# Moving the output scaling later, and five smaller edits, in a fused attention and two-layer kernel on one Trainium2 core

## The chip, the cores and the metric

The kernel runs on one core of a Trainium2 chip. The metric is the device time of one execution in microseconds (us). Each kernel was run several times on the same chip as the kernel before. A ratio is the mean time of one kernel's fast runs over that of the other's fast runs in the same rounds, so it is not quite the ratio of the medians that I also quote.

Names: PE is TensorE (matmul), PEld its weight loads, ACT ScalarE, DVE VectorE, POOL GpSimd, SP SyncE (SPq its sequencer).

## The reference, cut to what matters

```python
def mab(q, kv):                                   # attention with keys = values
    s = scale * (q @ kv.transpose(0, 2, 1))
    a = np.exp(s - s.max(-1, keepdims=True))
    a /= a.sum(-1, keepdims=True) + 1e-09
    return a @ kv
h = mab(I, x)                 # 32 inducing points attend to 12480 tokens, 4 batches
y = mab(x, h)                 # every token attends to the 32 rows of h
# then, for all 49920 tokens of 128 channels:
g = np.maximum(y @ w_in, 0) + alpha * np.minimum(y @ w_in, 0)     # 2048 wide
out = g @ w_out
```

## The kernel before: the parts that matter

The kernel folds the attention output into the first layer (`hW` = h times `w_in`), so that per group of 512 tokens it needs only the unnormalised attention weights `rep` (32 rows, repeated on four row groups). The second layer is split into a ReLU part (weights `W1`) and a linear part (`hA`), and the softmax denominator is divided out at the very end, by a multiply on DVE. I call that multiply the output scaling, or just the multiply.

A batch has 24 groups of 512 tokens and one short group of 192. A group is worked in four quarters, `j` = 0 to 3. In this text the "third quarter" is `j == 2` and the "fourth" is `j == 3`; the prediction numbers quarters by `j`. A quarter puts four first-layer matmuls into four banks of a ring of six PSUM banks (`fill`), ACT and DVE evict those banks with a ReLU, and one step later sixteen second-layer matmuls (`mm2`) add the result into one of two accumulators.

```python
def fill(st, g, j):
    ...
    for r in range(4):
        ps = bank()                        # next of six ring banks
        mm(ps[:, :w], st.hW[32*r : 32*r+32, j, :], rep[32*r : 32*r+32, :w])
    if j == 2:
        linear(st, lin_groups(st.b, g))    # even g: linear term of g AND g + 1
    ...
    for r, (ps, i) in enumerate(banks):    # a clock model picks the engine
        if ta <= td: pin(nc.scalar.activation(out=gt[:, r, :w], in_=ps[:, :w], func=RELU))
        else:        pin(nc.vector.tensor_relu(gt[:, r, :w], ps[:, :w]))
    return gt, done

def mm2(st, g, j, gt, done):
    acc = accs[(st.b * NG + g) % 2]        # two accumulators, taken in turn
    ...                                    # 16 matmuls acc += gt @ W1
    if j == NJ - 1 and st.b * NG + g > 0:
        finish(st, g)                      # DVE: ob = acc * rden; then the output DMA

# the loop: mm2 runs one quarter behind fill
for b, g, j in fills:
    gt, done = fill(states[b], g, j)
    for fn in tasks.pop((b * NG + g, j), []):
        fn()                               # next batch's scores, accumulation, ...
    if prev is not None:
        mm2(*prev)
    prev = (states[b], g, j, gt, done)
```

The tasks are work between the quarters: the next batch's scores and accumulation (its first attention), and the denominator matmuls, which sum the softmax weights of each token and take one more ring bank. PSUM is the memory into which the matmuls write.

The kernel holds each engine's instructions in program order (`pin`). `linear` of an even group `g` writes the accumulators of `g` and of `g + 1`. The accumulator of `g + 1` is the one that `finish(g - 1)` reads. So the second linear matmul, which writes that accumulator, cannot start before that multiply is done, and those behind it wait with it.

The softmax here doesn't subtract the row's maximum and nothing guards it: scores larger than these inputs give would overflow.

Of the kernel before, what the change touches and what calls it, by code (L numbers as in the profile page):

```python
# [15 lines left out]
P = 128  # L16
NB = 4
GRP = P * NB
NQ = 4
# [5 lines left out]
def kernel(  # L25
# [67 lines left out]
    def bank():  # L93
        i = ring_n[0] % RING
        ring_n[0] += 1
        clk["P"] = max(clk["P"], free[i])
        return ring[i]
# [87 lines left out]
    def e_xpose_pe(st, u):  # L185
        e1 = st.e1.pop(u)
        tp = bank()[:].bitcast(bf16)
        if u < NS:
            e1T = work.tile([P, NB, P], bf16, name="e1T", tag="e1T")
            for j in range(NB):  # L190
                pin(nc.tensor.transpose(
                    tp[:, j * P : (j + 1) * P], e1[:, j * P : (j + 1) * P], ident[:]
                ))
            pin(nc.vector.tensor_copy(  # L194
                out=e1T[:].rearrange("p j m -> p (j m)"), in_=tp[:, : NB * P]
            ))
        else:
            e1T = work.tile([P, JR, M], bf16, name="e1Tr", tag="e1Tr")
            for j in range(JR):
                pin(nc.tensor.transpose(  # L200
                    tp[:PR, j * M : (j + 1) * M], e1[:, j, :PR], ident[:M, :M]
                ))
            pin(nc.vector.tensor_copy(
                out=e1T[:PR].rearrange("p j m -> p (j m)"), in_=tp[:PR, : JR * M]
            ))
        st.e1T[u] = e1T
# [65 lines left out]

    def h_den(st):
        ps = bank()
        mm(ps[:, 0:1], fold[:], st.et[:])
        rh = work.tile([P, 1], f32, name="rh", tag="rh")
        pin(nc.vector.reciprocal(out=rh[:], in_=ps[:, 0:1]))
        st.fr = work.tile([P, P], f32, name="fr", tag="fr")
        pin(nc.vector.tensor_scalar_mul(out=st.fr[:], in0=fold[:], scalar1=rh[:]))


    def h_transpose(st):
        ps = bank()
        mm(ps[:, :P], st.hacc[:], st.fr[:])
        st.hT4 = work.tile([C, P], bf16, name="hT4", tag="hT4")
        pin(nc.vector.tensor_copy(out=st.hT4[:], in_=ps[:, :P]))
        st.hT = st.hT4[:, 0:M]

    def h_weights(st):
        ps = bank()  # L290
        for r in range(4):
            mm(
                ps[32 * r : 32 * r + 32, :], st.hT,
                w_in_b[:, r * NJ * P : (r + 1) * NJ * P],
            )
        st.hW = work.tile([P, NJ, P], bf16, name="hW", tag="hW")
        pin(nc.vector.tensor_copy(out=st.hW[:].rearrange("m j k -> m (j k)"), in_=ps[:]))

    def h_linear(st):
        pa = bank()  # L300
        mm(pa[:, :C], st.hT4[:], Amat[:])
        st.hA = work.tile([P, C], bf16, name="hA", tag="hA")
        pin(nc.vector.tensor_copy(out=st.hA[:], in_=pa[:, :C]))
# [52 lines left out]
    def b_den(st, s):  # L356
        e2 = st.e2.pop(s)
        ps = bank()
        clk["P"] += 240
        spent("D", 250)  # L360
        if s < NS:
            for j in range(NB):
                mm(ps[:, j * NQ : (j + 1) * NQ], e2[:, j * P : (j + 1) * P], pick[:])
            rd = work.tile([P, NB, NQ], f32, name="rd", tag="rd")
            pin(nc.vector.reciprocal(
                out=rd[:].rearrange("p j q -> p (j q)"), in_=ps[:, : NB * NQ]
            ))
        else:
            for j in range(JR):
                mm(ps[:PR, j : j + 1], e2[:, j * PR : (j + 1) * PR], pick[0:M, 0:1])  # L370
            rd = work.tile([PR, JR, 1], f32, name="rdr", tag="rdr")
            pin(nc.vector.reciprocal(
                out=rd[:].rearrange("p j q -> p (j q)"), in_=ps[:PR, :JR]
            ))
        st.rden[s] = rd


    def shape_of(g):
        return (P, NB) if g < NS * NQ else (PR, JR)

    def fill(st, g, j):
        pp, nb = shape_of(g)
        w = pp * nb
        rep = st.rep[g]
        gt = gt_pool.tile([P, 4, GRP], bf16, name="gt", tag="gt")
        banks = []
        for r in range(4):
            ps = bank()
            mm(
                ps[:, :w], st.hW[32 * r : 32 * r + 32, j, :], rep[32 * r : 32 * r + 32, :w]  # L390
            )
            banks.append((ps, (ring_n[0] - 1) % RING))
        if j == 2:
            linear(st, lin_groups(st.b, g))
        ca, cd = w * 0.75 + 96, w * 1.04 + 68
        ready = clk["P"] + 150 + w * 0.42
        clk["P"] = ready - 50 + (240 if j == 2 and lin_groups(st.b, g) else 0)
        done = ready
        for r, (ps, i) in enumerate(banks):
            ta, td = max(clk["A"], ready) + ca, max(clk["D"], ready) + cd  # L400
            if ta <= td:
                clk["A"] = free[i] = ta
                pin(nc.scalar.activation(out=gt[:, r, :w], in_=ps[:, :w], func=RELU))  # L403
            else:
                clk["D"] = free[i] = td
                pin(nc.vector.tensor_relu(gt[:, r, :w], ps[:, :w]))  # L406
            free[i] += 150
            done = max(done, free[i])
        return gt, done

    def mm2(st, g, j, gt, done):
        pp, nb = shape_of(g)
        acc = accs[(st.b * NG + g) % 2]
        clk["P"] = max(clk["P"], done) + 4 * nb * 57
        begun = g % 2 == 1 and st.b + g > 1
        for r in range(4):
            c = r * NJ + j
            for k in range(nb):
                mm(
                    acc[:pp, k, :], gt[:, r, k * pp : (k + 1) * pp], W1[:, c, :],  # L420
                    start=(j == 0 and r == 0 and k == 0 and not begun), stop=False,
                    skip_group_check=True,
                )
        if j == NJ - 1 and st.b * NG + g > 0:
            finish(st, g)



# [6 lines left out]
    def linear(st, groups):  # L435
        for k in range(NB):
            for r, g in enumerate(groups):
                pp, nb = shape_of(g)
                if k < nb:
                    mm(  # L440
                        accs[(st.b * NG + g) % 2][:pp, k, :],
                        st.rep[g][32 * r : 32 * r + 32, k * pp : (k + 1) * pp],
                        st.hA[32 * r : 32 * r + 32, :],
                        start=(r == 1 and k == 0), stop=False, skip_group_check=True,
                    )

    def finish(st, g):
        pp, nb = shape_of(g)
        acc = accs[(st.b * NG + g) % 2]
        s, q = divmod(g, NQ)  # L450
        rd = st.rden[s]
        rq = rd[:, :, q : q + 1]
        rbc = bass.AP(tensor=rq.tensor, offset=rq.offset, ap=[rq.ap[0], rq.ap[1], [0, C]])
        ob = ob_pool.tile([P, NB, C], f32, name="ob", tag="ob")
        pin(nc.vector.tensor_tensor(  # L455
            out=ob[:pp, :nb, :], in0=acc[:pp, :nb, :], in1=rbc, op=MULT
        ))
        spent("D", nb * C * 1.04 + 68, release=False)
        t0 = st.b * N + g * GRP
        last_one = (st.b, g) == (B - 1, NG - 1)  # L460
        pin((nc.sync if last_one else nc.gpsimd).dma_start(  # L461
            out=out[t0 : t0 + pp * nb, :].rearrange("(p j) c -> p j c", j=nb),
            in_=ob[:pp, :nb, :],
        ))
        st.rep.pop(g)
# [2 lines left out]

    order = [NS] + list(range(NS))
    st = new_batch(0)  # L470
    for u in order[:2]:
        a_load(st, u, pieces=2)
    ident = const.tile([P, P], bf16, name="ident")
    make_identity(nc, ident[:])
# [3 lines left out]
    nc.sync.dma_start(out=ind_f[:], in_=inducing)  # L478
    al_f = const.tile([KC, P], f32, name="al_f")
    nc.sync.dma_start(out=al_f[:], in_=moe_alpha.rearrange("(k p) -> k p", p=P))  # L480
    for u in order[2:]:
        a_load(st, u, pieces=2)
    w_in_b = const.tile([C, DFF], bf16, name="w_in_b")
    w_out_f = const.tile([P, KC, C], f32, name="w_out_f")
# [100 lines left out]
    warm(8)  # L585


    fills = [(b, g, j) for b in range(B) for g in range(NG) for j in range(NJ)]
    states = {0: st}
    tasks = {}  # L590

    def at(slot, fn, j=1):
        tasks.setdefault((slot, j), []).append(fn)
# [15 lines left out]
    for b in range(B):  # L609
# [6 lines left out]
        if b + 1 < B:  # L616
# [6 lines left out]
            for i, u in enumerate(order):  # L623
                k = base + i * (NG - 13) // NS
                at(k, lambda n=n, u=u: a_load(states[n], u))
                at(k + 3, lambda n=n, u=u: a_xpose(states[n], u))
                at(k + 5, lambda n=n, u=u: a_scores(states[n], u))
                at(k + 8, lambda n=n, u=u: a_accum(states[n], u))
            k = base + NG - 5
            at(k, lambda n=n: h_sum(states[n]))  # L630
            at(k, lambda n=n: h_den(states[n]), 3)
# [8 lines left out]
    for b, g, j in fills:  # L640
# [4 lines left out]
            mm2(*prev)  # L645
        prev = (states[b], g, j, gt, done)
    mm2(*prev)
    assert not tasks, tasks


# [28 lines left out]
```

## Time and profile before

| | |
|---|---|
| time | 617.5 us (617.35 to 618.03, 6 runs) |
| PE busy, PEld busy | 97%, 71% |
| DVE busy, ACT busy | 85%, 81% |
| an undisturbed quarter on PE | 1.33 us |
| stalls between the matmuls of the quarters | about 16.5 us (sum of the table of stalls below) |

These are two lines of the page of the kernel before: the span, and the busy time in us of each engine with its share of the span and its number of instructions.

```profile
span 615.2 us, 21846 instructions
...
PE 598.9 (97%) x9180; PEld 436.7 (71%) x9180; DVE 524.2 (85%) x935; ACT 500.8 (81%) x994; POOL 89.0 (14%) x151
```

PE seems full. It is not. The Trainium skill ("Perfetto Trace Analysis", section "Identifying the Most-Contended Engine") says that matmul busy time does not tell how close one is to the roofline, because pipelined matmuls look smaller in the trace, and that MFU (the share of the peak matmul rate) and weight-load busy time should be read instead. Weight loads cover only 71% of the span, but even an undisturbed quarter gives 75% (0.10 and 0.90 us of weight loads in 1.33 us), so most of the missing 29% is not stall.

The timeline shows where the rest is. Each line gives start and duration in us, engine, source line, operation, output<-inputs, shapes and count; the bracket is the engine's idle time before it and what ended that.

```profile
526.60 1.07 PE L105 MATMUL acc_88<-W_169,gt 128*128 128x128 bf16 x16
526.66 0.68 DVE L455 TENSOR_TENSOR ob<-acc_87,rd 128x512 f32<-128x512 f32 x1
526.74 0.60 ACT L403 ACTIVATE gt<-ring_85 128x512 bf16<-128x512 f32 x1 [0.24 <-ACT gt L403]
527.23 0.59 ACT L403 ACTIVATE gt<-ring_86 128x512 bf16<-128x512 f32 x1
527.26 0.68 DVE L406 TENSOR_SCALAR gt<-ring_81 128x512 bf16<-128x512 f32 x1
...
527.60 0.38 PE L105 MATMUL ring_83<-rep,hW 32*128 32x512 bf16 x1
...
527.88 0.37 PE L105 MATMUL ring_86<-rep,hW 32*128 32x512 bf16 x1
...
528.21 0.29 PE L105 MATMUL acc_88<-W_169,gt 128*128 128x128 bf16 x2
```

Read it as one slot of PE: the fills start at 527.60, but the fourth (ring_86) starts at 527.88. It needs ring_86 empty. That bank was the second one of the fill before, and ACT evicted it only from 527.23 to 527.82, because DVE was busy with the multiply (L455, 526.66) and could not take it. This slot also holds the linear matmuls, between 527.88 and 528.21 (left out here), which hide most of that wait: the slot loses 0.07 us. In a slot without them the same wait costs the full 0.26 us.

I cut the whole trace into such slots, from the first fill matmul of a quarter to the first fill matmul of the next, and subtracted what an undisturbed slot with the same contents takes. Undisturbed values are the shortest that recur: 1.327 us plain, 0.213 more with the linear matmuls, 0.33 more with scores or accumulation of the next batch, 0.10 more with the denominator matmuls. What is left over is the stall:

```
stall, us in the whole run       before   slots
after the multiply, no linear     5.3      43
with the linear matmuls           1.4      46
after the denominator matmuls     4.8      28
all other full slots              5.0     253
```

### The profile page before, as it was taken

To read this page: it belongs to the slowest core of one execution; us is meant where nothing else is said; L and a number is where in the kernel's file an instruction comes from. 1 tells how busy PE (TensorE), PEld (TensorE's weight loads), DVE (VectorE), ACT (ScalarE), POOL (GpSimd) and SP (SyncE) were. 2 spreads that over 40 slices of the span, in tenths; PEclk is the share of its full clock that TensorE was granted. 3 is DMA by queue.
4 is the path that set the end of the run, shared out by engine and by line. 5 is a ranking of instruction groups with operands and counts; after the bars stand their busy time and mean duration, and the time that the engine had idled before them with its cause. 6 is when DMAs were issued, how large, how long until landed. Compare 5 with 4: busy or idle time off the path is not lost.

```text
span 615.2 us, 21846 instructions
## 1 busy us (share of the span) xinstructions
PE 598.9 (97%) x9180; PEld 436.7 (71%) x9180; DVE 524.2 (85%) x935; ACT 500.8 (81%) x994; POOL 89.0 (14%) x151
## 2 busy tenths in 40 slices
PE   5799999999999999999999999999999999999996
PEld 4577777777777777777777777777777777777774
DVE  4688888889988888888988888888898888888885
ACT  2678888888888888888878888888888888888884
POOL 7241112101011111111011112110101011011010
PEclk9999999999999999999999999999999999999999
DMA  9824879652125598763122588864121221221211
GB/s 141 173 69 99 185 154 180 152 113 86 51 84 129 125 177 184 144 151 87 58 96 91 111 169 168 171 154 122 62 81 54 86 95 53 80 96 46 87 56 43
DMA packets 87458, 68.66 MB, mean 112 GB/s; under 512 B 53200, under 2 KB 80736, under 8 KB 87360
## 3 DMA queue, kind: packets, MB, share of 16 engines
q0 software_dynamic: 21456, 39.82, 26.2%
q1 hardware_dynamic: 65904, 27.45, 20.4%
q8 instruction: 72, 1.18, 0.8%
q14 instruction: 26, 0.21, 0.1%
HBM read 39.94 MB, written 28.62 MB: 111 GB/s over the span
## 4 chain that ended last, share of the span: by engine, by line
PE 95%; DVE 0%; ACT 0%; issue 0%
PE acc_87 L105 32%; PE acc_88 L105 32%; PE ring_82 L105 5%; PE ring_86 L105 5%; PE ring_84 L105 5%; PE ring_83 L105 5%; PE ring_81 L105 5%; PE ring_85 L105 5%; DVE gt L406 0%; ACT rep L342 0%; ACT gt L403 0%; PE ring_83 L543 0%; PE ring_81 L543 0%; DVE e1T L194 0%; DVE ob L455 0%
## 5 line engine op out<-in xcount | busy, mean ns | idle before, releaser
L105 PEld LDWEIGHTS <-gt 128*128 128x128 bf16 x6272 | 352.9, 98 | 83.0 <-issue 73.6
L105 PE MATMUL acc_87<-W_169,gt 128*128 128x128 bf16 (+1 forms) x3136 | 209.8, 220 | 0.0
L105 PE MATMUL acc_88<-W_169,gt 128*128 128x128 bf16 (+1 forms) x3136 | 209.6, 220 | 0.0
L461 POOL DMA_DIRECT2D out_dram<-ob x99 | 53.6, 541 | 501.6 <-DVE ob L455 482.2
L403 ACT ACTIVATE gt<-ring_86 128x512 bf16<-128x512 f32 (+1 forms) x159 | 92.2, 580 | 17.3 <-ACT gt L403 9.8
L403 ACT ACTIVATE gt<-ring_82 128x512 bf16<-128x512 f32 (+1 forms) x164 | 95.6, 583 | 12.2 <-ACT gt L403 7.9
L403 ACT ACTIVATE gt<-ring_84 128x512 bf16<-128x512 f32 (+1 forms) x151 | 88.5, 586 | 20.0 <-ACT gt L403 15.0
L105 PE MATMUL ring_84<-rep,hW 32*128 32x512 bf16 (+1 forms) x273 | 103.5, 379 | 0.0
L105 PE MATMUL ring_83<-rep,hW 32*128 32x512 bf16 (+1 forms) x273 | 103.0, 377 | 0.0
L105 PE MATMUL ring_81<-rep,hW 32*128 32x512 bf16 (+1 forms) x270 | 102.0, 378 | 0.7 <-ACT gt L403 0.4
L406 DVE TENSOR_SCALAR gt<-ring_81 128x512 bf16<-128x512 f32 (+1 forms) x139 | 91.3, 657 | 13.2 <-PE ring_83 L105 4.8
L105 PE MATMUL ring_86<-rep,hW 32*128 32x512 bf16 (+1 forms) x269 | 101.4, 377 | 0.1
L403 ACT ACTIVATE gt<-ring_85 128x512 bf16<-128x512 f32 x149 | 89.3, 599 | 12.3 <-ACT gt L403 8.4
L105 PE MATMUL ring_82<-rep,hW 32*128 32x512 bf16 (+1 forms) x258 | 97.4, 378 | 0.0
L105 PE MATMUL ring_85<-rep,hW 32*128 32x512 bf16 (+1 forms) x257 | 97.2, 378 | 0.0
L406 DVE TENSOR_SCALAR gt<-ring_83 128x512 bf16<-128x512 f32 (+1 forms) x128 | 84.3, 659 | 12.9 <-PE ring_85 L105 6.0
L406 DVE TENSOR_SCALAR gt<-ring_84 128x512 bf16<-128x512 f32 x122 | 83.6, 685 | 13.5 <-PE ring_86 L105 5.3
L403 ACT ACTIVATE gt<-ring_83 128x512 bf16<-128x512 f32 (+1 forms) x145 | 86.8, 598 | 10.3 <-ACT gt L403 7.5
L403 ACT ACTIVATE gt<-ring_81 128x512 bf16<-128x512 f32 x131 | 78.9, 602 | 19.4 <-ACT gt L403 13.0
L406 DVE TENSOR_SCALAR gt<-ring_85 128x512 bf16<-128x512 f32 (+1 forms) x108 | 72.1, 667 | 12.5 <-issue 5.4
L406 DVE TENSOR_SCALAR gt<-ring_86 128x512 bf16<-128x512 f32 x110 | 75.2, 684 | 7.4 <-ACT gt L403 3.0
L406 DVE TENSOR_SCALAR gt<-ring_82 128x512 bf16<-128x512 f32 x94 | 64.5, 687 | 10.1 <-issue 3.4
(299 smaller groups left out, 377.9 us busy)
## 6 DMA issues: line engine op xcount, KB each, us to landing
out_dram<-ob POOLq DMA_DIRECT2D x96, 256.0 KB, 2.6
rep<-e2d SPq DMA_DIRECT2D x92, 128.0 KB, 3.3
xn<-in_x_dram POOLq DMA_DIRECT2D x18, 512.0 KB, 6.0
xn<-in_x_dram POOLq DMA_DIRECT2D x12, 256.0 KB, 7.7
w_out_f<-in_moe_w_out_dram POOLq DMA_DIRECT2D x1, 1024.0 KB, 13.5
w_in_b<-in_moe_w_in_dram POOLq DMA_DIRECT2D x1, 512.0 KB, 11.4
xT<-xn SPq DMA_TRANSPOSE x18, 4.7
out_dram<-ob POOLq DMA_DIRECT2D x3, 96.0 KB, 2.0
```

Of the source, the lines that this page charges most:

```text
L105: return pin(nc.tensor.matmul(o, lhsT, rhs, start=start, stop=stop, **kw))
L403: pin(nc.scalar.activation(out=gt[:, r, :w], in_=ps[:, :w], func=RELU))
L406: pin(nc.vector.tensor_relu(gt[:, r, :w], ps[:, :w]))
L461: pin((nc.sync if last_one else nc.gpsimd).dma_start(out=out[t0 : t0 + pp * nb, :].rearrange("(p j) c -> p j c", j=nb), in_=ob[:pp, :nb, :],))
```

## The change

Its intent is to let PE run its slots without waiting for banks: scale the output later, behind the first two evictions of the next quarter, so that the second bank is evicted at once; do the short group with two chunks of 192 columns in one bank, which halves its evictions; let the head's loads start earlier; and give ACT a copy for which DVE was late. The clock model that deals evictions to ACT and DVE was corrected, and two tasks of the next batch moved to other quarters. Cut to its core:

```diff
     def fill(st, g, j):
+        pp, nb, cp = shape_of(g)           # cp: 1, or 2 in the short group
         for r in range(4):
             ps = bank()
-            mm(ps[:, :w], st.hW[32*r : 32*r+32, j, :], rep[...])
+            for i in range(cp):
+                mm(ps[:, i*t : (i+1)*t], st.hW[32*r : 32*r+32, j*cp + i, :], rep[...])
-        if j == 2:
+        lin = j == 2 // cp and lin_groups(st.b, g)
+        if lin:
             linear(st, ...)
@@ the evictions
         for r, (ps, i) in enumerate(banks):
+            if r == 2:
+                while held:
+                    finish(*held.pop())
@@ end of mm2
-        if j == NJ - 1 and st.b * NG + g > 0:
-            finish(st, g)
+        if j == NJ // cp - 1 and st.b * NG + g > 0:
+            held.append((st, g))
@@ the clock model (further numbers of this kind cut)
-        ready = clk["P"] + 150 + w * 0.42
+        ready = clk["P"] + 240 + w * 0.42
@@ one copy of the head
+            if u in order[-3:-2]:
+                pin(nc.scalar.copy(out=dst, in_=tp[:, : NB * P]))
@@ the head: loads ahead of the identity set-up
-    for u in order[:2]:
+    for u in order[:3]:
         a_load(st, u, pieces=2)
@@ tasks of the next batch (default quarter is j = 1)
-                at(k + 5, lambda n=n, u=u: a_scores(states[n], u))
-                at(k + 8, lambda n=n, u=u: a_accum(states[n], u))
+                at(k + 5, lambda n=n, u=u: a_scores(states[n], u), 0)
+                at(k + 8, lambda n=n, u=u: a_accum(states[n], u), 2)
```

More of the change, by code (lines that the diff above doesn't have):

```diff
@@ L193, in e_xpose_pe @@
                 ))
-            pin(nc.vector.tensor_copy(
-                out=e1T[:].rearrange("p j m -> p (j m)"), in_=tp[:, : NB * P]
-            ))
+            dst = e1T[:].rearrange("p j m -> p (j m)")
+            if u in order[-3:-2]:
+                pin(nc.scalar.copy(out=dst, in_=tp[:, : NB * P]))
+            else:
+                pin(nc.vector.tensor_copy(out=dst, in_=tp[:, : NB * P]))
         else:
@@ L274, in h_den @@
         ps = bank()
+        clk["P"] += 250
+        spent("D", 500)
         mm(ps[:, 0:1], fold[:], st.et[:])
@@ L283, in h_transpose @@
         ps = bank()
+        clk["P"] += 300
+        spent("D", 250)
         mm(ps[:, :P], st.hacc[:], st.fr[:])
@@ L290, in h_weights @@
         ps = bank()
+        clk["P"] += 320
+        spent("D", 600)
         for r in range(4):
@@ L300, in h_linear @@
         pa = bank()
+        clk["P"] += 80
+        spent("D", 250)
         mm(pa[:, :C], st.hT4[:], Amat[:])
@@ L358, in b_den @@
         ps = bank()
-        clk["P"] += 240
+        clk["P"] += 130
         spent("D", 250)
@@ L378, in shape_of @@
     def shape_of(g):
-        return (P, NB) if g < NS * NQ else (PR, JR)
+        return (P, NB, 1) if g < NS * NQ else (PR, JR, 2)
+    held = []
     def fill(st, g, j):
-        pp, nb = shape_of(g)
-        w = pp * nb
+        pp, nb, cp = shape_of(g)
+        t = pp * nb
+        w = t * cp
         rep = st.rep[g]
@@ L388, in fill @@
             ps = bank()
-            mm(
-                ps[:, :w], st.hW[32 * r : 32 * r + 32, j, :], rep[32 * r : 32 * r + 32, :w]
-            )
+            for i in range(cp):
+                mm(
+                    ps[:, i * t : (i + 1) * t],
+                    st.hW[32 * r : 32 * r + 32, j * cp + i, :],
+                    rep[32 * r : 32 * r + 32, :t],
+                )
             banks.append((ps, (ring_n[0] - 1) % RING))
-        if j == 2:
-            linear(st, lin_groups(st.b, g))
+        lin = j == 2 // cp and lin_groups(st.b, g)
+        if lin:
+            linear(st, lin)
         ca, cd = w * 0.75 + 96, w * 1.04 + 68
-        ready = clk["P"] + 150 + w * 0.42
-        clk["P"] = ready - 50 + (240 if j == 2 and lin_groups(st.b, g) else 0)
-        done = ready
+        ready = clk["P"] + 240 + w * 0.42
+        clk["P"] = ready - 135 + (240 if lin else 0)
+        done = []
         for r, (ps, i) in enumerate(banks):
+            if r == 2:
+                while held:
+                    finish(*held.pop())
             ta, td = max(clk["A"], ready) + ca, max(clk["D"], ready) + cd
@@ L407, in fill @@
             free[i] += 150
-            done = max(done, free[i])
+            done.append(free[i])
         return gt, done
     def mm2(st, g, j, gt, done):
-        pp, nb = shape_of(g)
+        pp, nb, cp = shape_of(g)
         acc = accs[(st.b * NG + g) % 2]
-        clk["P"] = max(clk["P"], done) + 4 * nb * 57
-        begun = g % 2 == 1 and st.b + g > 1
+        t = clk["P"]
         for r in range(4):
-            c = r * NJ + j
-            for k in range(nb):
-                mm(
-                    acc[:pp, k, :], gt[:, r, k * pp : (k + 1) * pp], W1[:, c, :],
-                    start=(j == 0 and r == 0 and k == 0 and not begun), stop=False,
-                    skip_group_check=True,
-                )
-        if j == NJ - 1 and st.b * NG + g > 0:
-            finish(st, g)
+            t = max(t, done[r]) + cp * nb * 57
+        clk["P"] = t + 85
+        begun = (g % 2 == 1 and st.b + g > 1) or cp > 1
+        for r in range(4):
+            for i in range(cp):
+                c = r * NJ + j * cp + i
+                for k in range(nb):
+                    k0 = (i * nb + k) * pp
+                    mm(
+                        acc[:pp, k, :], gt[:, r, k0 : k0 + pp], W1[:, c, :],
+                        start=(j == 0 and r == 0 and i == 0 and k == 0 and not begun),
+                        stop=False, skip_group_check=True,
+                    )
+        if j == NJ // cp - 1 and st.b * NG + g > 0:
+            held.append((st, g))
     def lin_groups(b, g):
@@ L437, in linear @@
             for r, g in enumerate(groups):
-                pp, nb = shape_of(g)
+                pp, nb, cp = shape_of(g)
                 if k < nb:
@@ L443, in linear @@
                         st.hA[32 * r : 32 * r + 32, :],
-                        start=(r == 1 and k == 0), stop=False, skip_group_check=True,
+                        start=((r == 1 or cp > 1) and k == 0), stop=False, skip_group_check=True,
                     )
     def finish(st, g):
-        pp, nb = shape_of(g)
+        pp, nb, _ = shape_of(g)
         acc = accs[(st.b * NG + g) % 2]
@@ L480 @@
     nc.sync.dma_start(out=al_f[:], in_=moe_alpha.rearrange("(k p) -> k p", p=P))
-    for u in order[2:]:
+    for u in order[3:]:
         a_load(st, u, pieces=2)
@@ L585 @@
     warm(8)
-    fills = [(b, g, j) for b in range(B) for g in range(NG) for j in range(NJ)]
+    fills = [(b, g, j) for b in range(B) for g in range(NG)
+             for j in range(NJ // shape_of(g)[2])]
     states = {0: st}
@@ L647 @@
     mm2(*prev)
+    finish(*held.pop())
     assert not tasks, tasks
```

## The prediction

> **What bounds the kernel now.** The page shows PE 97% busy, but the Trainium skill ("Perfetto Trace Analysis", opening note) calls matmul busy time a bad metric because matmuls are pipelined. The timeline agrees: stalls hide inside the 97%. From about 30 us on, the kernel is a chain of some 400 slots on TensorE: four first-layer matmuls into four of six ring banks (0.32 us), then sixteen second-layer matmuls (1.00 us). An undisturbed slot takes 1.33 us. Measuring slots in the timeline from first fill matmul to first fill matmul, I find the stalls as spread between a slot's first and fourth fill matmul: about 22 us in all. The fourth matmul waits for a bank that an eviction still holds.
>
> - After output scaling (the 0.68 us DVE multiply of an accumulator): the multiply goes first on DVE, so the second bank is evicted second on ScalarE (0.59 us, 0.49 start to start). The slot takes 1.58 instead of 1.33; the sum over the run is about 6 us. Where the linear term shares the slot it takes 1.60, against 1.54 undisturbed (about 1.5 us).
> - After the denominator matmuls, which take an extra bank: 1.49, about 4.5 us. The change leaves these.
> - Two slots after a scores task of the next batch: 1.49, about 4 us; its Exp plus accumulator read (0.8 us) precedes evictions on ScalarE.
>
> **What the change does.**
> 1. Late scaling: the second bank now goes to DVE before the multiply, so its bank is free in time. Gain about 6 us in the slots without the linear term. In the slots with it, the linear matmuls write the accumulator that the multiply reads. Worked out from the timeline, eviction (0.19 + 0.61) and multiply (0.68) end 1.48 us after the second-layer matmuls begin, but PE is ready at 1.31. I expect a new wait of about 0.2 us in about 45 slots: cost 5 to 8 us.
> 2. Moving scores and accumulation to quarters 0 and 2: gain about 3 us of the 4, but accumulation no longer gives slack ahead of the linear term (counted above).
> 3. Short group, two chunks to a bank: 16 evictions of 192 columns become 8 of 384 (ACT about 0.39, DVE 0.48, interpolated from 192 and 512), and four fills become two. About 0.5 to 0.7 us per group, 2.3 us in all.
> 4. Head: identity behind three loads delays DVE's set-up by about 1.5 us, but PE then waits 2.1 us for the second unit's data anyway, and DMA is 90% busy from 3 us on, so the last load (21.9 us) hardly moves. The copy on ScalarE shortens PE's 0.86 us wait at 23.6. Together 0.3 us.
> 5. The scheduling model's corrected numbers re-deal ACT and DVE in some slots: unknown, up to 2 us either way.
>
> Sum: -6 -3 -2.3 -0.3 +6, about -6 to -7 us: 611 us. Range 604.5 to 615.5. Chances: faster by over 2% 0.11, within 2% 0.88, slower 0.01.
>
> **What would show it.** Right: slots after scaling without linear at 1.33; the slots with linear at 1.7 or more, PE waiting there for the DVE multiply in the chain and the waits; short-group stretch near 4.1 us instead of 4.6; after-denominator slots still 1.49; first group still starting near 29.5 us. Wrong on 1 if linear slots stay at 1.54 to 1.60: then 605. Wrong on 2 if plain slots keep 0.18 us spreads.
>
> **What would make it wrong.** The linear wait missing (faster), the re-dealing helping after-denominator slots (faster), or three evictions on ScalarE after scaling delaying the next fill (slower).

## The result, and the profile after

The changed kernel takes 617.42 us (616.92 to 617.50, 6 runs) against 617.51 us; the ratio is 0.9995, with a 95% interval of 0.9983 to 1.0008. Nothing was gained. The same lines of the page:

```profile
span 615.2 us, 21629 instructions
...
PE 593.5 (96%) x9179; PEld 432.0 (70%) x9180; DVE 529.4 (86%) x918; ACT 500.0 (81%) x979; POOL 89.0 (14%) x151
```

PE's weight loads moved from 71% to 70%. The page gives no hint that anything happened. The slots do:

```
stall, us in the whole run       before   after   change
after the multiply, no linear     5.3      0.1     -5.2
with the linear matmuls           1.4     12.2    +10.8
after the denominator matmuls     4.8      5.0     +0.2
all other full slots              5.0      0.7     -4.3
short groups of three batches    (4.63    4.04 each) -1.8
head, to the first fill          29.50   28.88     -0.6
last short fill start to the
  multiply of the group before    1.30    2.24     +0.9
sum                                                 0.0
```

The last line needs a word. In both kernels the run's end hangs on the multiply of the group before the last, through its output write, as the sixth and seventh experiments show. That multiply starts at 606.28 us before and 606.26 us after, which is the same time, and the seven terms add up to that. (The first 18.2 us from the first fill on are left out of the classes of slots; they take the same time in both.)

So the change did all that it set out to do. The bank stalls that it aimed at are gone. And 10.8 us of a new wait took it all back. This is the timeline after, for the same slots as in the lines of before:

```profile
525.86 1.07 PE L105 MATMUL acc_88<-W_169,gt 128*128 128x128 bf16 x16
...
526.05 0.69 DVE L428 TENSOR_SCALAR gt<-ring_86 128x512 bf16<-128x512 f32 x1
...
526.66 0.68 DVE L482 TENSOR_TENSOR ob<-acc_87,rd 128x512 f32<-128x512 f32 x1
526.86 0.38 PE L105 MATMUL ring_83<-rep,hW 32*128 32x512 bf16 x1
...
526.87 0.39 PE L105 MATMUL ring_86<-rep,hW 32*128 32x512 bf16 x1
...
527.09 0.21 PE L105 MATMUL acc_88<-hA,rep 32*128 32x128 bf16 x1
527.34 0.69 DVE L428 TENSOR_SCALAR gt<-ring_83 128x512 bf16<-128x512 f32 x1
527.39 0.21 PE L105 MATMUL acc_87<-hA,rep 32*128 32x128 bf16 x1
...
527.70 0.29 PE L105 MATMUL acc_88<-W_169,gt 128*128 128x128 bf16 x2
```

The second bank (ring_86) now goes to DVE at 526.05, and all four fills start at 526.86 together. The multiply follows at 526.66. The first linear matmul (acc_88, the group in progress) starts at 527.09. The second one writes acc_87, which the multiply still reads, and it starts at 527.39, when DVE is free again. Only at 527.70 do the second-layer matmuls start: 1.84 us after the ones before (525.86), where an undisturbed slot takes 1.54. Here is such a slot from the same trace, in which the multiply ends in time because another task stands in front of it:

```profile
309.51 1.07 PE L105 MATMUL acc_88<-W_169,gt 128*128 128x128 bf16 x16
...
309.92 0.68 DVE L482 TENSOR_TENSOR ob<-acc_87,rd 128x512 f32<-128x512 f32 x1
...
310.74 0.21 PE L105 MATMUL acc_87<-hA,rep 32*128 32x128 bf16 x1
...
311.05 1.07 PE L105 MATMUL acc_88<-W_169,gt 128*128 128x128 bf16 x16
```

Undisturbed, the second linear matmul starts 1.23 us after the second-layer matmuls (309.51 to 310.74); held, 1.53 us (525.86 to 527.39). That is the 0.30 us. From there to the next second-layer matmul it is 0.31 us in both.

The chain of work that ended last, in order of time, names the culprit (start and duration in us, engine, tile, line):

```profile
526.93 0.32 PE ring_83 L105
...
527.25 0.04 PE ring_86 L105
...
527.29 0.05 DVE ob L482
527.35 0.04 issue
527.39 0.21 PE acc_87 L105
...
527.77 0.55 PE acc_88 L105 x8
```

The chain goes from the fills to "DVE ob", the multiply, and from there to the linear matmul on acc_87. In the same stretch of the kernel before, the chain stays on PE throughout. The view of waits is less clear. Its columns are who waited for whom, us in total, times, longest. First the kernel before:

```profile
...
PEld L105 <- issue: 102.7, 396, 0.9
```

And after:

```profile
...
PEld L105 <- issue: 109.1, 422, 0.9
```

The wait for the multiply does not appear under its own name. It sits in "PEld L105 <- issue", which grew from 102.7 to 109.1 us. Where a wait is not named there, the chain and the timeline must be read.

The short group did get shorter. These lines give the busy time of each engine in two stretches: the short group with the full quarters mixed into it, and the full slot after it. Before:

```profile
318.71:323.34 4.63, 4.63 (x72) 3.55 (x70) 3.54 (x10) 3.10 (x11) 0.54 (x1) 1.00 0.16 60
323.34:325.00 1.66, 1.66 (x22) 1.09 (x21) 1.66 (x4) 1.66 (x5) 0.13 (x1) 1.00 0.00 0
```

After:

```profile
319.40:323.44 4.04, 4.04 (x73) 3.32 (x72) 3.43 (x7) 3.24 (x8) 0.54 (x1) 1.00 0.02 6
323.44:324.76 1.32, 1.32 (x22) 0.99 (x20) 1.25 (x3) 1.05 (x3) 0.00 (x0) 1.00 0.52 196
```

That is 6.29 against 5.36 us.

### The profile page after: what moved, and what is told of

Its sections match the earlier page's. It is cut to its first block, busy times and chain, and to the rows that moved or that the text cites. A ratio compares the mean times of both kernels' runs of the same rounds, so it can differ in the third digit from the quotient of the medians.

```text
span 615.2 us, 21629 instructions
## 1 busy us (share of the span) xinstructions
PE 593.5 (96%) x9179; PEld 432.0 (70%) x9180; DVE 529.4 (86%) x918; ACT 500.0 (81%) x979; POOL 89.0 (14%) x151
## 4 chain that ended last, share of the span: by engine, by line
PE 94%; DMA 2%; POOL 1%; DVE 1%; issue 1%; ACT 0%; DVEq 0%; POOLq 0%
PE acc_87 L105 33%; PE acc_88 L105 33%; PE ring_82 L105 5%; PE ring_86 L105 5%; PE ring_84 L105 5%; PE ring_83 L105 5%; PE ring_81 L105 4%; PE ring_85 L105 4%; DMA xn<-in_x_dram 2%; POOL xn L136 1%; DVE ob L482 1%; DVE gt L428 0%; POOL xnr L141 0%; PE ring_84 L167 0%; ACT rep L352 0%
## 5 line engine op out<-in xcount | busy, mean ns | idle before, releaser
L105 PEld LDWEIGHTS <-gt 128*128 128x128 bf16 x6272 | 352.4, 98 | 76.0 <-issue 70.0
L105 PE MATMUL acc_87<-W_169,gt 128*128 128x128 bf16 (+1 forms) x3136 | 208.9, 220 | 0.0
L105 PE MATMUL acc_88<-W_169,gt 128*128 128x128 bf16 (+1 forms) x3136 | 208.8, 220 | 0.0
L425 ACT ACTIVATE gt<-ring_84 128x512 bf16<-128x512 f32 (+1 forms) x158 | 94.5, 598 | 19.5 <-ACT gt L425 15.8
L425 ACT ACTIVATE gt<-ring_86 128x512 bf16<-128x512 f32 x153 | 91.4, 597 | 15.8 <-ACT gt L425 11.4
L425 ACT ACTIVATE gt<-ring_82 128x512 bf16<-128x512 f32 (+1 forms) x149 | 89.1, 598 | 16.1 <-ACT gt L425 10.9
L105 PE MATMUL ring_84<-rep,hW 32*128 32x512 bf16 (+1 forms) x270 | 101.1, 378 | 0.0
L105 PE MATMUL ring_83<-rep,hW 32*128 32x512 bf16 (+1 forms) x269 | 101.1, 379 | 0.0
L105 PE MATMUL ring_86<-rep,hW 32*128 32x512 bf16 (+1 forms) x267 | 100.4, 379 | 0.0
L105 PE MATMUL ring_81<-rep,hW 32*128 32x512 bf16 (+1 forms) x265 | 99.6, 379 | 0.7 <-ACT gt L425 0.5
L425 ACT ACTIVATE gt<-ring_81 128x512 bf16<-128x512 f32 x144 | 86.5, 601 | 16.3 <-ACT gt L425 11.8
L105 PE MATMUL ring_85<-rep,hW 32*128 32x512 bf16 (+1 forms) x266 | 99.5, 378 | 0.0
L105 PE MATMUL ring_82<-rep,hW 32*128 32x512 bf16 (+1 forms) x263 | 98.9, 379 | 0.0
L425 ACT ACTIVATE gt<-ring_83 128x512 bf16<-128x512 f32 x141 | 84.5, 599 | 11.4 <-ACT gt L425 6.3
L425 ACT ACTIVATE gt<-ring_85 128x512 bf16<-128x512 f32 (+1 forms) x138 | 82.7, 600 | 12.5 <-ACT gt L425 7.9
```

The costliest lines, as they stand in the source:

```text
L105: return pin(nc.tensor.matmul(o, lhsT, rhs, start=start, stop=stop, **kw))
```

## The experiments

Two theories were on the table.

- W: TensorE waits for the late multiply in front of the linear matmuls, and this alone took the gain back.
- R, the rival: ACT and DVE, at 81% and 85%, are together the real limit. Time saved in one slot then has to come back in another, and moving one wait only moves the loss.

All outputs are right. The table gives the time, the ratio to the kernel before of the same rounds, and its interval.

| run | edit | time, us | ratio | 95% interval |
|---|---|---|---|---|
| a1_linear_q3 | after + linear matmuls in the fourth quarter | 602.23 | 0.9758 | 0.9744 to 0.9773 |
| a2_early_before_linear | after + multiply early only ahead of the linear quarter | 609.08 | 0.9872 | 0.9856 to 0.9889 |
| a3_multiply_at_once | after, late scaling undone | 615.25 | 0.9968 | 0.9954 to 0.9983 |
| a4_accum_q1 | after + accumulation back in the second quarter | 611.88 | 0.9914 | 0.9899 to 0.9928 |
| a7_linear_q3_tail | a1 + last but one output on SyncE's queue | 598.19 | 0.9689 | 0.9675 to 0.9704 |
| a6_tail_queue | after + last but one output on SyncE's queue | 613.75 | 0.9941 | 0.9926 to 0.9955 |
| b4_late_only | before + late scaling | 617.54 | 0.9999 | 0.9982 to 1.0016 |
| b1_short_only | before + short group | 614.30 | 0.9949 | 0.9934 to 0.9964 |
| b2_identity_only | before + identity set-up behind three loads | 617.56 | 1.0003 | 0.9989 to 1.0017 |
| b3_copy_only | before + one copy on ACT | 617.69 | 1.0006 | 0.9994 to 1.0019 |
| a5_multiply_last | after + multiply behind all four evictions | 658.04 | 1.0663 | 1.0648 to 1.0677 |
| b5_late_and_q3 | before + late scaling + linear in the fourth quarter | 607.93 | 0.9847 | 0.9831 to 0.9863 |

### 1. Take the wait away: linear matmuls one quarter later

```diff
-        lin = j == 2 // cp and lin_groups(st.b, g)
+        lin = j == 3 // cp and lin_groups(st.b, g)
```

> Changed kernel, but the linear matmuls move from the third quarter of the even groups to the fourth, one slot later, where the late multiply is long done. Theory W (TensorE waits for the late multiply in front of the linear matmuls; the changed trace has 46 such slots with 0.27 us over an undisturbed 1.54, 10.9 us in all): that wait vanishes. The denominator matmuls share the fourth quarter, so their slot gets 0.2 us longer and the 0.18 us bank stall after them (28 slots, 5.0 us) should go too: 601 to 607 us. Rival R (ScalarE and DVE are the joint limit, and what is saved in one slot comes back in another): 614 to 618 us, with new stalls elsewhere.

Measured: 602.23 us. The stall in the linear slots fell from 12.2 to 0.6 us, and the one after the denominator matmuls from 5.0 to 1.8. No other class of slot grew by more than 0.1 us, so R fell here. DVE and ACT went up in share because they do the same work in less time. The page of this run, and the timeline around one linear slot:

```profile
span 600.3 us, 21629 instructions
...
PE 582.3 (97%) x9179; PEld 434.9 (72%) x9180; DVE 530.7 (88%) x918; ACT 499.9 (83%) x979; POOL 89.0 (15%) x151
```

```profile
492.55 0.68 DVE L482 TENSOR_TENSOR ob<-acc,rd 128x512 f32<-128x512 f32 x1
...
494.08 0.40 PE L105 MATMUL ring<-rep,hW 32*128 32x512 bf16 x4
...
494.31 0.39 PE L105 MATMUL acc<-hA,rep 32*128 32x128 bf16 x8
...
494.62 0.25 PE L105 MATMUL ring<-pick,e 128*128 128x4 bf16 x4
...
494.74 1.05 PE L105 MATMUL acc<-W,gt 128*128 128x128 bf16 x16
...
495.73 0.40 PE L105 MATMUL ring<-rep,hW 32*128 32x512 bf16 x4
```

The multiply (L482, 492.55) is over long before the linear matmuls start at 494.31. The slot from 494.08 to 495.73 holds linear and denominator matmuls in 1.65 us, about the sum of its parts (1.33 + 0.21 + 0.10). The next fills start together at 495.73, with no stall after the denominators: the longer slot seems to give the third bank time to be evicted before the next fill wants it.

### 2. Take it away in another way: multiply early only where linear follows

```diff
         for r, (ps, i) in enumerate(banks):
-            if r == 2:
+            if r == (0 if g % 2 == 0 and cp == 1 else 2):
                 while held:
                     finish(*held.pop())
```

> Changed kernel, but the multiply goes ahead of the four evictions (as before) only in the slot in front of the linear matmuls, and stays late elsewhere. W: the slots with the linear term fall from 1.81 to about 1.60 (the value before), 46 x 0.21 = 9.7 us less: 606 to 610 us. R: within 2 us of 617.

Measured: 609.08 us. Linear slots without another task take 1.60 us in the mean, as before the change, and their class's stall is 3.2 us. The slots after the multiply stay at 1.33. W holds.

### 3. Undo the late scaling

```diff
-            held.append((st, g))
+            finish(st, g)
```

> Changed kernel with the late scaling undone everywhere: the multiply follows its last matmuls at once. W: the linear slots lose their wait (-10 us), the slots after the multiply without linear term get their bank stall back (about 46 x 0.26 = +12 us, now also where the moved scores no longer cover it): 616 to 621 us, and the last multiply but one comes earlier (up to -1 us). R: also about 617, so the slots decide, not the sum: W wants linear slots near 1.60 and slots after the multiply near 1.58.

Measured: 615.25 us, a little under the range. The slots were as W wanted in direction: linear stalls 12.2 to 3.0 us, stalls after the multiply 0.1 to 7.2 us. The latter came to 7.2, not 12; I had multiplied 0.26 by all slots, but not all of them stalled in full (0.17 in the mean of 43). The kernel with the short group alone (experiment 8) takes 614.30 us, so all else in the change (moved tasks, clock model, head), without the late scaling, gained nothing. The slots say why: from the kernel of experiment 8 to this one the other full slots lose 2.5 us of stall, but those after the multiply and those with the linear matmuls gain 1.9 and 1.4.

### 4. Put other work in front of the wait

```diff
-                at(k + 8, lambda n=n, u=u: a_accum(states[n], u), 2)
+                at(k + 8, lambda n=n, u=u: a_accum(states[n], u))
```

> Changed kernel with the next batch's accumulation moved back from the third to the second quarter, that is between the multiply and the linear matmuls. W: its 0.33 us of matmuls cover the wait of 0.3 us in the 21 slots it shares with the linear term, so 21 x 0.3 = 6 us less: 610 to 613 us, linear slots of the first three batches at 1.54, those of the last batch still at 1.84. R: within 2 us of 617.

Measured: 611.88 us. Linear slots that follow another task (21 an accumulation, 3 scores) take 1.55 us in the mean, the other 22 take 1.82. So the change's move of the accumulation had uncovered half of the wait.

### 5. Make the suspected wait longer

```diff
         for r, (ps, i) in enumerate(banks):
-            if r == 2:
-                while held:
-                    finish(*held.pop())
             ...
+        while held:
+            finish(*held.pop())
         return gt, done
```

> Changed kernel with the multiply still later, behind all four evictions of the slot. Theory W: the multiply then ends 0.6 us later (one more eviction on DVE, 0.61 start to start), and each of the 46 linear slots waits 0.6 us more: 46 x 0.6 = 27 us, 638 to 648 us, linear slots near 2.4, slots without linear term unchanged at 1.33. Rival R (ScalarE and DVE the joint limit): the same evictions are done, so within 3 us of 617.

Measured: 658.04 us, more than expected. The linear slots did as W said: 2.40 us without another task, and 39.6 us of stall against 12.2, which is 27.4 more. The rest I had wrong: slots after the multiply did not stay at 1.33 but took 1.57 (12.4 us in all), since the multiply now ran into the next quarter's evictions and brought the old bank stall back. The two sums (39.6 - 12.2 + 12.4 - 0.1 = 39.7) explain the 40.6 us. Timeline of one linear slot, where the wait is now named:

```profile
524.37 0.40 PE L105 MATMUL ring<-rep,hW 32*128 32x512 bf16 x4
524.60 0.21 PE L105 MATMUL acc<-hA,rep 32*128 32x128 bf16 x1
524.76 0.68 DVE L480 TENSOR_TENSOR ob<-acc,rd 128x512 f32<-128x512 f32 x1
...
525.49 0.38 PE L105 MATMUL acc<-hA,rep 32*128 32x128 bf16 x7 [0.68 <-DVE ob L480]
...
525.80 1.07 PE L105 MATMUL acc<-W,gt 128*128 128x128 bf16 x16
```

One linear matmul at 524.60, then 0.68 us of idle PE until DVE's multiply ends, then the other seven.

### 6 and 7. Where the end of the run hangs

The changed kernel's last matmuls were done 1.6 us earlier than before, and yet both spans are 615.2 us. The ends of the two timelines, before:

```profile
606.28 0.69 DVE L455 TENSOR_TENSOR ob<-acc_87,rd 128x512 f32<-128x512 f32 x1 [0.29 <-PE acc_87 L105]
...
607.26 0.54 POOL L461 DMA_DIRECT2D out_dram<-ob  x1 [4.89 <-DVE gt L406]
...
609.35 0.42 DVE L455 TENSOR_TENSOR ob<-acc_88,rdr 96x256 f32<-96x256 f32 x1 [0.41 <-PE acc_88 L105]
609.80 0.32 SPq L461 DMA_DIRECT2D out_dram<-ob  x1
```

And after:

```profile
606.26 0.68 DVE L482 TENSOR_TENSOR ob<-acc_87,rd 128x512 f32<-128x512 f32 x1
...
607.23 0.54 POOL L488 DMA_DIRECT2D out_dram<-ob  x1 [4.61 <-DVE ob L482]
607.71 0.42 DVE L482 TENSOR_TENSOR ob<-acc_88,rdr 96x256 f32<-96x256 f32 x1 [0.77 <-PE acc_88 L105]
608.16 0.32 SPq L488 DMA_DIRECT2D out_dram<-ob  x1
```

The very last multiply moved from 609.35 to 607.71, but the one before it (606.28, 606.26) did not, nor did its output, the last DMA that GpSimd issues (607.26, 607.23). The trace's records that the timeline leaves out show a drain on GpSimd that begins with this issue and lasts 7.17 us in both:

```
                                before    after    a6      a7
last GpSimd DMA issue           607.26   607.23   603.20  587.44
GpSimd drain, us                  7.17     7.17     7.09    7.09
drain ends                      614.41   614.38   610.26  594.51
last output write has landed    611.60   610.27   611.10  595.66
end of the span                 615.20   615.17   612.20  596.75
```

```diff
-        last_one = (st.b, g) == (B - 1, NG - 1)
+        last_one = st.b == B - 1 and g >= NG - 2      # goes to SyncE's queue
```

> Changed kernel with only the last output write but one moved to SyncE's queue. Theory D: 612.5 to 614.5 us (last landing at 610.3 us in the changed trace, then about 1 us to the end). Rival: 617 us.

> Changed kernel with the linear matmuls in the fourth quarter (602.2 us in an earlier run) and the last output write but one sent from SyncE's queue instead of GpSimd's, as the very last already is. Theory D: in both traces GpSimd spends 7.17 us in a drain from its last DMA issue on, and that, not the last write, ends the run; the last GpSimd issue would then come about 5 us earlier and the last write's landing would set the end, some 3.8 us sooner: 597.5 to 600 us. Rival: the drain only waits for the last data, so nothing changes (601.5 to 603).

Measured: 613.75 and 598.19 us. With the last GpSimd issue one group earlier, the end follows the last landing by about 1 us, and no longer the drain. In the changed kernel 1.6 us gained in the tail (609.35 to 607.71) seem to have been hidden under the drain; the kernel before was not run with this edit. The page of a7, the fastest kernel here, 3.1% under the kernel before:

```profile
span 596.7 us, 21630 instructions
...
PE 581.9 (98%) x9180; PEld 434.3 (73%) x9180; DVE 530.6 (89%) x918; ACT 499.8 (84%) x979; POOL 88.5 (15%) x150
```

### 8 to 11. The parts alone

The short group alone (its lines of the diff above, on the kernel before):

> Kernel before with the short group's two chunks to a bank alone. In the traces the short group and the full slots after it take 0.93 us less in each of the three batches that have a successor (6.29 against 5.36 us); in the last batch the end hangs on the multiply of the group before it, which hardly moves: 614.0 to 615.5 us. If the stretch were paid back elsewhere: 617.

Measured: 614.30 us. The gain of the short group is real and is not paid back.

The late scaling alone:

```diff
-            finish(st, g)
+            held.append((st, g))
@@ fill, at the evictions
+            if r == 2:
+                while held:
+                    finish(*held.pop())
```

> Kernel before with the late scaling alone (behind the second of the next four evictions), nothing else. Theory W: slots after the multiply lose 5.2 us of bank stalls; in the 25 linear slots that no accumulation covers the wait for the multiply adds 25 x 0.25 = 6 us; the last multiply but one comes some 0.4 us later: 616.5 to 619.5 us, linear slots without accumulation in front of them at 1.8, with it at 1.54.

Measured: 617.54 us. Stalls after the multiply 5.3 to 0.3 us, linear stalls 1.4 to 5.8 us. Linear slots with another task in the slot before take 1.55 us, the others 1.79. By itself the late scaling is worth nothing.

The two edits of the head:

> Kernel before with the identity set-up behind three loads alone. The first layer's first matmul started at 29.50 us before and 28.88 after, but at 29.2 to 29.75 in four other runs of the same head, so the traces settle little. If the earlier loads help: up to 0.4 us less; if the head hangs on the last load: within 0.2 us of the kernel before.

> Kernel before with the one copy of the head moved to ScalarE alone. The wait it shortens is 0.86 us of TensorE just after the last load; predicted 0.1 to 0.3 us less. Any change of more than 0.5 us would be a surprise.

Measured: 617.56 and 617.69 us, ratios 1.0003 and 1.0006. Neither shows a gain. The first fill starts at 30.16 us in the trace of the one and at 29.24 in that of the other. In the traces with the head of before it lies between 29.24 and 29.95, in those with the changed head between 28.88 and 29.75, so the 0.6 us between the two traces of before and after is within what the same head does from run to run.

### 12. The smallest edit that works

The kernel before with the late scaling (as above) and the linear matmuls in the fourth quarter:

```diff
-        if j == 2:
+        if j == 3:
             linear(st, lin_groups(st.b, g))
```

> Kernel before with two edits only: late scaling (alone it was worth nothing, 617.5 us) and the linear matmuls in the fourth quarter. Theory W, with the stalls read from the traces: 5.2 us of bank stalls after the multiply go, about 1 us in the linear slots, about 3 us after the denominator matmuls (as in the first experiment, 5.0 to 1.8): 607 to 609.5 us. Theory R: 616 us or more.

Measured: 607.93 us. Two edits of a few lines give 1.5%. The first alone was worth nothing; the second alone was not run, so what it brings without the late scaling is not known. The stalls after the multiply are 0.4 us, linear 0.7, after the denominators 1.1. The other full slots keep 4.4 us; that part needed the moved tasks or the corrected clock model.

## Why the prediction was wrong, point by point

The prediction said 611 us and a range of 604.5 to 615.5. Measured: 617.42. The mechanism was right, but the sum was 5.6 us too low. The new wait was mis-sized by 4.8 us (10.8 for 6), and the tail cost 0.9 us that was not foreseen; the other terms nearly cancel.

- Where the kernel loses time: right. The fourth fill waits for a bank. The four classes of slot named are the ones in which the stalls are, though the "about 22 us in all" counts spreads that cost nothing (16.5 us by slots).
- "Gain about 6 us in the slots without the linear term": right, 5.2 us measured, and 0.1 of stall left.
- "I expect a new wait of about 0.2 us in about 45 slots: cost 5 to 8 us": this is the step that failed. The wait came where it was expected, but it was 0.30 us (in a slot with no other task 1.84 against 1.54) in 40 of the 46 slots, with 0.04 us in three and none in three that follow another task; in sum 10.8 us more than before. The end of the multiply was predicted exactly: 1.48 us after the second-layer matmuls begin, 1.48 measured (525.86 to 527.34). Wrong was "PE is ready at 1.31": the held matmul starts at 1.23 where nothing holds it, before the fills have ended. And PE resumes only 0.05 us after the multiply, at 1.53. So the 0.17 us of the prediction missed 0.08 at the start of the wait and 0.05 at its end. The sum was also too kind to its own term: 0.2 us in 45 slots is 9 us, or 7.5 beyond the 1.5 that these slots lost before, and 6 was entered.
- "Gain about 3 us of the 4" from the moved tasks: the class fell by 4.3 us, part of it in the slot behind the short group. But experiments 3 and 8 show that moved tasks, clock model and head together gain nothing without the late scaling; what they take from the other slots comes back after the multiply and in the linear slots. That the accumulation gave slack was right, and experiment 4 measured it: 5.5 us between the changed kernel's 617.42 and 611.88.
- "2.3 us in all" for the short group: 0.59 us in the group itself (4.63 to 4.04), as predicted. That the sum is near, 2.8 us, is luck: the full slot after the group gave another 0.34, not predicted, and only three batches count. In the fourth the multiply of the group before the last came 0.9 us later (2.24 against 1.30; 0.8 of it is the late scaling, since experiment 3 has 1.41), which GpSimd's drain passes on to the end of the run. I had not looked at what ends the run.
- "Together 0.3 us" for the head: not shown. Both edits alone are within the noise.
- "Unknown, up to 2 us either way" for the clock model: left open. No run isolates it from the moved tasks.
- The sum as written (-6 -3 -2.3 -0.3 +6) is -5.6, so 611.9 us and not 611. With the measured terms it is 0.0.
- What would show it: the linear slots at 1.7 or more (1.84), plain slots at 1.33, after-denominator slots still 1.48 to 1.49 and the short stretch at 4.0: all seen. The wait was to be seen in the chain and the waits; it is in the chain, but the view of waits hides it under "issue".

What stays open: how much of the 4.3 us in the other full slots is due to the moved scores and how much to the clock model, and what GpSimd's drain of 7.17 us waits for.

## What to carry to other kernels

When you delay an operation to take it out of one wait, list everything that reads or overwrites its buffer, and move the first of those along with it; here moving the linear matmuls by one quarter turned a gain of nothing into 2.4%. Size a new wait from the moment at which the held work starts when nothing holds it, read from a trace, and not from when the work ahead of it should be done; here that alone was 0.08 of 0.30 us. And before counting a gain in the last stage, look at what ends the run: it need not be the last result.

## What the Trainium skill lacked or had wrong

- GpSimd's drain at the end. "VectorE: DVE Perf Modes", section "The DRAIN you can't avoid", tells two kinds of drain apart, a pipeline flush after each DVE operation and the runtime's own of about 12 ns on all five engines. The one that ended the run before and after (at 614.41 of 615.20 us) is neither: the trace puts it on the line of kernel.py that encloses the whole program. It lasts 7.09 to 7.54 us in all traces and begins with GpSimd's last DMA issue. I found no page that gives its length.
- The issuing engine of a DMA. "DMA: Bandwidth & Descriptors", section "Issuing engines are not separate DMA queues", says that spreading issues over engines only saves the sequencer's time, which is usually small. Moving one output write of 256 KB from GpSimd to SyncE took the ratio from 0.9995 to 0.9941 (617.42 to 613.75 us), for the reason above.
- "Perfetto Trace Analysis", section "Identifying the Most-Contended Engine", held: over before, a1 and a7 PE's busy share went 97, 97, 98%, while weight-load share rose 71, 72, 73% as the time fell by 3.1%. Even that is a weak signal: the weight-load time itself stayed at 434.3 to 436.7 us, so its share restates the span, and it did not tell before from after (71, 70%), whose stalls differ in kind but not in sum.
- No page that I read says how to size a wait of TensorE on an accumulator that another engine still reads. Here PE resumed 0.05 us after the multiply's end, and the held matmuls started at 1.53 us instead of 1.23, so that the wait was 0.30 us and not the 0.17 from the predicted figures.
